# Linear attention and a gated MLP on one core: queries scaled at the cast, a new order of the first loads, filler matmuls, and no two-operand work on GpSimd

## The chip, the cores and the metric

The kernel runs on one core of a Trainium2 chip. The metric is the device time of one execution in microseconds. A core has five engines that run side by side: TensorE (PE in the profile; its weight loads are PEld), VectorE (DVE), ScalarE (ACT), GpSimd (POOL) and SyncE (SP). SP, ACT and POOL also issue DMA transfers, each into a queue of its own. Matmuls write to the eight banks of PSUM.

## The reference

Decayed linear attention in blocks of 64 rows, for 4 batches, 8 heads, 768 rows and a head size of 64, then an MLP over the 3072 rows of the result (512 to 2048 to 512, SiLU between).

```python
for b in range(nb):                                   # 12 blocks of 64 rows
    intra = (qb @ kb.T * Dmask) @ vb                  # lam**(i-j) for i >= j
    inter = (qb * lam_pow) @ kv_state                 # lam**(i+1)
    out[block] = intra + inter
    kv_state = lam**64 * kv_state + (kb * rev_pow).T @ vb
x = out.transpose(0, 2, 1, 3).reshape(B * S, H * D)   # 3072 x 512
h = x @ w_in                                          # 2048 wide
result = (h / (1 + exp(-h))) @ w_out
```

## The kernel before, in words

**Units and sets.** The rows of a batch are cut into six units of 128 rows, 24 in all. Two units are loaded as a set, three loads each (keys, queries, values, `raw`, 512 KB in float32). Sets 0 to 3 hold units 0 and 1 of one batch each and are "paired" (`prepare_2`, `first_2`, `second_2`); sets 4 to 11 hold one unit of two batches (`prepare`, `first_part`, `second_part`).

**Attention of one set.** Keys and queries are cast to bf16 (`kq`, on DVE or ACT, L313 and L315), values are scaled by powers of lambda (`vd`, L320, on DVE or POOL). TensorE turns `kq` into `kqT` (L442, through a PSUM bank `tr` and a copy) for sets 0 to 3; the rest are turned by a DMA transpose that SP issues (L622). TensorE then forms the states (`d_ps`, L463 and L647) and the scores (`st_ps`, L514 and L657). DVE masks the scores (`st`). The states run through a short chain on DVE (`y`, `xf`, `yf`), and the result is copied into block-diagonal tiles (`xe`, L313, L315, L317). TensorE adds scores times values ("outs", L538 and L679) and states times queries ("inter", L543 and L687) in `x_ps`. DVE takes that out of PSUM and multiplies it by `lam_xe`, the queries' power of lambda, into `xt`. In `first_2` the states stand ahead of the scores, and a chain (`after("b", ...)`) keeps that order on TensorE.

**MLP.** For each group of units, `product1` multiplies `xt` by w_in (L830, output `h_ps`) and ACT applies SiLU into `g` (L839). A group is one paired set (256 columns per matmul) or four units (512). For units 0 to 7, `product2_plain` multiplies `g` by w_out (L861, `o_ps`). For units 8 to 23, `product2` forms seven products in place of eight out of sums and differences of the blocks of `g` and of w_out (L1072). These sums (`s`, and `g` in place) are DVE's, except one of the four, which goes to POOL (`BY_POOL`). The last group's first product is formed the same way (`product1_spared`, L944).

**Weights.** w_in and w_out come in four quarters each, cast to bf16 on the way, issued by POOL (L364, L367). `SEQUENCE` sets the order of the first loads: "s0 i0 s1 i1 i2 s2 i3 o0 s3 o1 o2 o3 s4", where s is a set (issued by SP), i a quarter of w_in, o a quarter of w_out. The first quarter after a set is held by a gate: a small POOL copy (L331) that reads the set's first load, so POOL issues the quarter only once that load is there.

**Order.** Every piece of work is a task with a key (its priority), the engines that can do it and an assumed time on each, the tasks it depends on, and its buffers (`Buf`, from pools whose sizes stand in `POOLS`; "two", "one" and "att" are tickets that hold back how much is open at once). The `Planner` plays the tasks through with these times, a model of the load queues and the moment at which each engine begins, and writes down an order for each engine. The instructions are issued in that order; each engine works through its own list strictly in order.

Of the kernel before, what the change touches and what calls it, by code (L numbers as in the profile page):

```python
# [37 lines left out]
class Planner:  # L38

    LAT = {"PE": 0.23, "ACT": 0.06, "DVE": 0.06, "POOL": 0.08, "SP": 0.0}  # L40
    BEGIN = {"PE": 0.8, "ACT": 8.3, "DVE": 4.5, "POOL": 4.7, "SP": 0.8}
    FIRST, LAST, AHEAD = {"SP": 1.9, "ACT": 1.15, "POOL": 2.5}, 1.0, 0.75

    def __init__(self, pools):
        self.pools = {n: list(range(c)) for n, c in pools.items()}
        self.tasks = []

    def add(self, key, on, fn, deps=(), bufs=(), nbytes=0, kind=None, prior=(), late=0.0):
        key = key if isinstance(key, tuple) else (key,)
        t = Task(key, on, fn, deps, list(bufs) + [b.with_ for b in bufs if b.with_], nbytes, kind, prior, late)  # L50
        for b in t.bufs:
            b.left += 1
        self.tasks.append(t)
        return t

    def order(self):
# [14 lines left out]
        seq = 0  # L71
# [48 lines left out]
        while len(out) < len(self.tasks):  # L120
# [9 lines left out]
            for e in free:  # L130
# [8 lines left out]
                while ready[e]:  # L139
# [12 lines left out]
                    mine = now + t.on[e]  # L152
                    if any(max(free[o], now) + d < mine - 1e-9 for o, d in t.on.items() if o != e):
                        kept.append((key, i, t))
                        continue
# [4 lines left out]
                if took is None:  # L160
                    continue
# [5 lines left out]
                free[e] = now + t.on[e]  # L167
# [21 lines left out]
def kernel(  # L189
# [70 lines left out]
    row_i = const.tile([128, U], mybir.dt.int32, name="row_i")  # L260
    nc.gpsimd.iota(row_i, pattern=[[1, U]], base=-64, channel_multiplier=0)
# [20 lines left out]
    pose_2 = const.tile([128, 2], F32, name="pose_2")  # L282
    for a in range(2):
        nc.vector.tensor_scalar(pose_2[:, a:a + 1], iota_2, -1.0, 64.0 - a, op0=AL.mult, op1=AL.add)
    pose = const.tile([128, 1], F32, name="pose")
    nc.vector.tensor_scalar(pose, iota_p, -1.0, 64.0, op0=AL.mult, op1=AL.add)
    row = const.tile([128, U], F32, name="row")
    nc.vector.tensor_copy(row, row_i)
# [6 lines left out]
    lam_v = const.tile([128, H], F32, name="lam_v")  # L295
    lam_xe = const.tile([128, NP, U], F32, name="lam_xe")
    lam_be = const.tile([128, NP], F32, name="lam_be")
    lam_v2 = const.tile([128, H, 2], F32, name="lam_v2")
    for a in range(2):
        nc.scalar.activation(lam_v2[:, :, a], log_all, AF.Exp, scale=pose_2[:, a:a + 1])  # L300
    nc.scalar.activation(lam_v, log_all, AF.Exp, scale=pose[:, 0:1])
    for a in range(NP):
        nc.scalar.activation(lam_xe[:, a, :], row, AF.Exp, scale=log_lam[:, a:a + 1])
# [26 lines left out]
    def gated(key, load, i, tile):  # L330
        pool_task(add(key, {"POOL": 0.15}, lambda e: nc.gpsimd.tensor_copy(gate[:, i:i + 1], tile()), deps=load,  # L331
                      prior=pool_last[-1:]))
# [3 lines left out]
    raw = {}  # L336

    def load_set(key, si):
        n, b = sets[si][0]
        nb = 2  # L340
        rs = [Buf("ra" if si in (0, 3) else "rb") for _ in range(3)]
# [4 lines left out]
        def go(e, i):  # L346
            if n < PAIRED:
                tile_of(rs[i], [128, H, 2, 64], F32, "raw")
                nc.sync.dma_start(out=rs[i].tile.rearrange("p h e d -> p h (e d)"), in_=x[i])
            else:  # L350
                nc.sync.dma_start(out=tile_of(rs[i], [128, 2 * H, 64], F32, "raw"), in_=x[i])

        for i in range(3):
            ts.append([add((key, i), {"SP": 0.55}, lambda e, i=i: go(e, i), bufs=[rs[i]], nbytes=0.524,
                           kind=WIDE if n < PAIRED else SMALL, late=0.3 if si < FRESH else 3.0)])
        raw[si] = rs, ts
# [3 lines left out]
    def load_w(key, what, j):  # L360
        def go(e):
            if what == "i":
                cs = slice(512 * j, 512 * j + 512)
                nc.gpsimd.dma_start(out=w_in_bf[:, :, cs], in_=w_in_r[:, :, cs])  # L364
            else:
# [3 lines left out]
        wload[what, j] = pool_task(add((key, 0), {"POOL": 0.8}, go, [], [], 1.0486,  # L369
                                       LARGE, prior=pool_last[-1:], late=1.0))  # L370

    last, unit = None, None
    for m, x in enumerate(SEQUENCE.split() + [f"s{i}" for i in range(len(sets))]):
        j = int(x[1:])
        if x[0] == "s":
            if j not in raw:
                load_set(m - 100, j)
                unit = j
        else:
            if last != unit:  # L380
                rs, loads = raw[unit]
                gated((m - 100, -1), loads[0], unit, lambda b=rs[0]: b.tile[:, 0, 0, 0:1] if len(b.tile.shape) == 4 else b.tile[:, 0, 0:1])
                last = unit
            load_w(m - 100, x[0], j)
# [25 lines left out]
    def key_of(si):  # L410
        u = rank[sets[si][0]]
        return u - 4.0 if sets[si][0][0] == 0 else u - LEAD

    def prepare_2(o, rs, lk, lq, lv):
# [5 lines left out]
        def cast(e, i, a):  # L420
            copy(e, o.kq_of()[:, i, :, a], rs[i].tile[:, :, a, :].rearrange("p (m h) d -> p m h d", h=2))

        o.ck = [[add((s - 1.0, i), {"DVE": 0.43, "ACT": 0.63}, lambda e, i=i, a=a: cast(e, i, a), deps=(lk, lq)[i],
                     bufs=[rs[i], o.kq]) for a in range(2)] for i in range(2)]
# [7 lines left out]
        o.cv = [add((s - 0.8, 0), {"DVE": 0.7}, lambda e, a=a: scale_v(e, a), deps=lv, bufs=[rs[2], o.vd]) for a in range(2)]  # L432
# [19 lines left out]
    def first_2(o):  # L452
# [13 lines left out]
        td = add((s - 0.6, 0), {"PE": 0.45}, states, deps=o.cv + o.ck[0], bufs=d_ps + [o.kq, o.vd])  # L466
        after("b", td)
# [13 lines left out]
        def blocks(xe, i, src, t, buf):  # L481
            def go(e, r):
                if xe.tile is None:
# [6 lines left out]
        t0 = add((s - 0.9, 3), {"DVE": 0.42}, lambda e: tt(e, small(xf), d_ps[0].tile, rate, AL.mult), deps=[td], bufs=[d_ps[0], xf])  # L490
        o.xe_ready = blocks(o.xe_in, 0, lambda: xf.tile, t0, xf)
        t1 = add((s - 0.9, 4), {"DVE": 0.42}, lambda e: tt(e, small(y), d_ps[1].tile, xf.tile, AL.add), deps=[td, t0],
                 bufs=[d_ps[1], xf, y])
        t2 = add((s - 0.9, 5), {"DVE": 0.42, "POOL": 0.7}, lambda e: tt(e, xf_of(), y.tile, rate, AL.mult), deps=[t1], bufs=[y, xf_n])
        xf_t.append(t2)
        xe_t += blocks(xe_n, b0 % 2, xf_of, t2, xf_n)

# [6 lines left out]
        o.st_of = st_of  # L504
        deps = [t for t in o.turned]
        o.masked = []
        for g in range(2):
# [11 lines left out]
            for p in range(2):  # L519
# [5 lines left out]
                o.masked.append(add((s - 0.9, 0), {"DVE": 0.69}, mask, deps=[ts], bufs=[st_ps[g][p], o.st2[p]]))  # L525
        after("m", o.masked)

    def second_2(o):
# [21 lines left out]
        for c in range(2):  # L550
            def evac(e, c=c):
                tl = tile_of(xt[gi], [128, KI, 256], BF16, "xt")
                dst = tl[:, :, 128 * c:128 * c + 128].rearrange("p m (c e) -> p m e c", e=2)
                tt(e, dst, x_ps[c].tile, lam_xe.rearrange("p m (c e) -> p m e c", e=2), AL.mult)

            xt_done[gi].append(add((s - 0.9, 6), {"DVE": 0.7}, evac, deps=[(t0, t1)[c]], bufs=[x_ps[c], xt[gi]]))

    def prepare(si):
# [7 lines left out]
        o.kq, o.kqT, o.vd, o.st = Buf("kq"), Buf("kqT"), Buf("vd"), Buf("st")  # L566
# [6 lines left out]
        def kq_of():  # L573
            return tile_of(o.kq, [128, nb, 2, NP, 2, 64], BF16, "kq")

        def kqT_of():
            return tile_of(o.kqT, [128, nb, 2, NP, U], BF16, "kqT")
# [9 lines left out]
        def cast(e, j, i):  # L587
            src = rs[i].tile[:, j * H:j * H + H, :].rearrange("p (m h) d -> p m h d", h=2)
            dst = kq_of()[:, j, i]
            copy(e, dst, src)  # L590

        ck = [[add((s - 1.0, i), {"DVE": 0.43, "ACT": 0.63}, lambda e, j=j, i=i: cast(e, j, i), deps=(lk, lq)[i],
                   bufs=[rs[i], o.kq]) for i in range(2)] for j in range(nb)]
        after("k", [t for ts in ck for t in ts])
# [4 lines left out]
        cv = [add((s - 0.8, 0), {"DVE": 0.7} if si < FRESH else {"POOL": 1.25, "DVE": 0.7}, lambda e, j=j: scale_v(e, j),  # L599
# [5 lines left out]
        if si < TURNED:  # L605
            for j in range(nb):
                bank = Bank(fills=False)

                def turn(e, j=j, bank=bank):
                    t = tile_of(bank, [128, 2, NP, U], BF16, "tr")  # L610
                    for i in range(2):
                        for m in range(NP):
                            nc.tensor.transpose(t[:, i, m, :], kq_of()[:, j, i, m], ident)

                tr = add((s - 0.7, j), {"PE": 0.46}, turn, deps=ck[j], bufs=[bank, o.kq])
                for i in range(2):
                    o.turned.append(add((s - 1.0, 2), {"DVE": 0.43, "ACT": 0.6},
                                        lambda e, j=j, i=i, bank=bank: copy(e, kqT_of()[:, j, i], bank.tile[:, i]),
                                        deps=[tr], bufs=[bank, o.kqT]))
        else:  # L620
            def dma_turn(e):
                nc.sync.dma_start_transpose(kqT_of().rearrange("p b i m s -> p (b i m) s"),  # L622
                                            kq_of().rearrange("p b i m h d -> p (b i m h d)"))
# [4 lines left out]
    def first_part(o):  # L628
# [12 lines left out]
        def states(e):  # L641
            for j in range(nb):
                for m in range(NP):
                    for c in halves_of_d:
                        r = halves[c]
                        for p, rp in enumerate(halves):
                            nc.tensor.matmul(d_of(c)[rp, j, m, :], lhsT=o.kq_of()[r, j, 0, m, p, :],  # L647
# [3 lines left out]
        def scores(e):  # L651
            for j in range(nb):
                for m in range(NP):
                    for p, rp in enumerate(halves):
                        t = tile_of(st_ps[p], [128, nb, NP, 64], F32, "st_ps")
                        for c, r in enumerate(halves):
                            nc.tensor.matmul(t[r, j, m, :], lhsT=o.kqT_of()[rp, j, 0, m, r], rhs=o.kqT_of()[rp, j, 1, m, r],  # L657
# [6 lines left out]
    def second_part(o):  # L664
# [18 lines left out]
        def inter(e):  # L683
            for c in range(2):
                for j in range(nb):
                    for m in range(NP):
                        nc.tensor.matmul(x_of(c)[:, j, m, :], lhsT=o.xe[c].tile[:, (bs[0] + j) % 2, m, :],  # L687
                                         rhs=o.kqT_of()[:, j, 1, m, halves[c]],
# [484 lines left out]
```

## Time and profile before

| what | us |
|---|---|
| time, median of 3 runs (lowest, highest) | 207.66 (207.39, 208.27) |
| profiled execution | 207.82 |
| its span, first to last instruction | 206.1 |
| PE busy | 187.0 (91%) |
| DVE busy | 134.8 (65%) |
| ACT busy | 107.4 (52%) |
| POOL busy | 52.4 (25%) |
| mean granted clock of TensorE | 0.989 |

The page cuts the span into 40 slices of 5.15 us and gives the busy share of each engine in each slice as one digit, in tenths. PEclk is the granted TensorE clock in tenths of full speed. A chain row gives the start, the length and the work that the end of the program hung on. In the timeline a bracket gives the idle time ahead of an instruction and what ended it. Matmuls overlap, so the mean duration of one is longer than the time that it takes from its neighbours. The queue q0 carries what POOL issues, q1 what SP issues, q10 what ACT issues; q0's bytes are counted after the cast to bf16.

### The profile page before, as it was taken

The numbers are of one execution on the slowest core, as the hardware profiler recorded it, in microseconds if no ns is written. First come the engines' busy times: TensorE is split into PE (matmuls) and PEld (weight loads), VectorE is DVE, ScalarE is ACT, GpSimd is POOL, SyncE is SP. The second block draws the span as 40 slices with busy tenths as digits, with TensorE's granted clock in tenths as the row PEclk, the third lists the DMA queues.
The fourth block names the chain that finished last, engine by engine and source line by source line (L and its number), as shares of the span: only waits on it lengthen the run. The fifth ranks groups of instructions, "written<-read, shape, count | busy, mean of one in ns | idle before, by whom it ended". The sixth has DMA issues, their size and how long they took to land.

```text
span 206.1 us, 5719 instructions
## 1 busy us (share of the span) xinstructions
PE 187.0 (91%) x2445; PEld 132.9 (64%) x2464; DVE 134.8 (65%) x249; ACT 107.4 (52%) x195; POOL 52.4 (25%) x76
## 2 busy tenths in 40 slices
PE   0459399999999999999999999998999999999993
PEld 0347288786667565544578648474675778888882
DVE  6488632767950467716989953999758995665411
ACT  3637267874336453375734492745615453766420
POOL 7231400401130111222565013346003221222200
PEclk9999889999999999999999999999999999999999
DMA  3999999999999999999999999905101110102213
GB/s 99 292 253 260 228 222 265 235 199 214 228 238 249 156 216 231 238 219 195 263 213 234 203 213 240 244 7 117 39 3 54 51 54 0 54 0 102 88 52 118
DMA packets 88617, 33.92 MB, mean 165 GB/s; under 512 B 67088, under 2 KB 87568, under 8 KB 88592
## 3 DMA queue, kind: packets, MB, share of 16 engines
q1 hardware_dynamic: 79232, 23.60, 57.3%
q0 software_dynamic: 4224, 4.19, 12.2%
q10 hardware_dynamic: 5136, 5.77, 8.7%
q8 instruction: 19, 0.31, 0.7%
q14 instruction: 6, 0.05, 0.1%
HBM read 27.27 MB, written 6.29 MB: 163 GB/s over the span
## 4 chain that ended last, share of the span: by engine, by line
PE 82%; DMA 8%; DVE 7%; issue 1%; ACT 0%; POOL 0%; POOLq 0%; DVEq 0%
PE h_ps L830 31%; PE o_ps L1072 22%; PE o_ps L861 13%; PE h_ps L944 6%; DMA w_in_bf<-in_moe_w_in_dram 5%; DMA raw<-in_k_dram 3%; PE x_ps L687 2%; DVE s L320 2%; PE tr L442 2%; DVE g L320 1%; PE d_ps L647 1%; PE x_ps L679 1%; PE st_ps L657 1%; PE x_ps L538 1%; DVE kq L315 1%
## 5 line engine op out<-in xcount | busy, mean ns | idle before, releaser
L830 PE MATMUL h_ps<-xt,w_in_bf 128*128 128x256 bf16 (+1 forms) x439 | 75.7, 322 | 4.7 <-DMA w_in_bf<-in_moe_w_in_dram 3.3
L839 ACT ACTIVATE g<-h_ps 128x512 bf16<-128x512 f32 x80 | 47.1, 594 | 45.7 <-PE h_ps L830 45.0
L830 PEld LDWEIGHTS <-w_in_bf 128*128 128x128 bf16 x448 | 43.7, 99 | 30.1 <-DMA w_in_bf<-in_moe_w_in_dram 3.5
L861 PE MATMUL o_ps<-w_out_bf,g 128*128 128x512 bf16 x118 | 29.7, 379 | 0.6 <-issue 0.2
L320 POOL TENSOR_TENSOR s<-g,s 128x512 bf16<-128x512 bf16 x16 | 19.0, 1188 | 43.1 <-DVE s L320 26.8
L320 DVE TENSOR_TENSOR st<-st_ps,tri 128x512 bf16<-128x512 f32 x32 | 20.5, 681 | 11.2 <-PE st_ps L657 11.2
L1072 PEld LDWEIGHTS <-g 128*128 128x128 bf16 x256 | 24.9, 98 | 4.4 <-ACT g L839 0.3
L320 DVE TENSOR_TENSOR xt<-x_ps,lam_xe 128x512 bf16<-128x512 f32 x24 | 15.9, 699 | 15.2 <-PE x_ps L687 9.5
L1072 PEld LDWEIGHTS <-s 128*128 128x128 bf16 x192 | 18.7, 98 | 2.6
L861 PEld LDWEIGHTS <-g 128*128 128x128 bf16 x128 | 12.1, 98 | 12.0
L320 POOL TENSOR_TENSOR vd<-raw,lam_v 128x512 bf16<-128x512 f32 x10 | 13.3, 1334 | 25.1 <-DMA raw<-in_v_dram 19.7
L313 ACT ACTIVATE kq<-raw 128x512 bf16<-128x512 f32 x27 | 16.2, 621 | 2.1 <-DMA raw<-in_q_dram 1.6
L320 DVE TENSOR_TENSOR osb<-o_ps,m 128x512 f32<-128x512 f32 (+1 forms) x15 | 8.7, 583 | 10.9 <-ACT m L313 6.8
L1072 PE MATMUL o_ps<-wsum,g 128*128 128x256 bf16 x128 | 15.3, 272 | 0.0
L1072 PE MATMUL o_ps<-w_out_bf,s 128*128 128x256 bf16 x128 | 15.3, 273 | 0.0
L442 PE MATMUL tr<-ident,kq 128*128 128x128 bf16 x64 | 7.0, 260 | 8.8 <-POOL gate L331 6.9
L1072 PE MATMUL o_ps<-w_out_bf,g 128*128 128x256 bf16 x128 | 15.0, 273 | 0.0
L320 DVE TENSOR_TENSOR s<-g 128x512 bf16<-128x512 bf16 x16 | 8.2, 510 | 10.4 <-ACT g L839 6.6
L313 ACT ACTIVATE m<-o_ps 128x512 f32<-128x512 f32 (+1 forms) x14 | 7.0, 503 | 11.4 <-PE o_ps L1072 11.4
L320 DVE TENSOR_TENSOR vd<-raw,lam_v 128x512 bf16<-128x512 f32 x14 | 9.2, 681 | 5.0 <-DMA raw<-in_v_dram 5.0
L313 ACT ACTIVATE osb<-o_ps 128x512 f32<-128x512 f32 (+1 forms) x12 | 6.7, 562 | 10.4 <-PE o_ps L861 6.5
L315 DVE CAST kq<-raw 128x512 bf16<-128x512 f32 x21 | 9.1, 451 | 3.8 <-DMA raw<-in_k_dram 2.0
(88 smaller groups left out, 215.1 us busy)
## 6 DMA issues: line engine op xcount, KB each, us to landing
raw<-in_k_dram SPq DMA_DIRECT2D x12, 512.0 KB, 8.2
raw<-in_q_dram SPq DMA_DIRECT2D x12, 512.0 KB, 8.5
raw<-in_v_dram SPq DMA_DIRECT2D x12, 512.0 KB, 8.0
out_dram<-osb ACTq DMA_DIRECT2D x20, 256.0 KB, 3.6
w_in_bf<-in_moe_w_in_dram POOLq DMA_DIRECT2D x4, 512.0 KB, 10.0
w_out_bf<-in_moe_w_out_dram POOLq DMA_DIRECT2D x4, 512.0 KB, 11.7
out_dram<-osb ACTq DMA_DIRECT2D x4, 128.0 KB, 1.7
out_dram<-osb SPq DMA_DIRECT2D x4, 128.0 KB, 1.7
```

The source lines that it names most:

```text
L313: nc.scalar.activation(o, i, AF.Copy)
L315: nc.vector.tensor_copy(o, i)
L320: (nc.vector if e == "DVE" else nc.gpsimd).tensor_tensor(o, a, b, op=op)
L442: nc.tensor.transpose(t[:, m, a], o.kq_of()[:, i, m, a], ident)
L538: nc.tensor.matmul(t[rh, m], lhsT=o.vd_of()[r, 2 * m + h, a, :], rhs=o.st_of(h)[r, m, a], start=m == 0 and a == 0, stop=True, skip_group_c ...
L647: nc.tensor.matmul(d_of(c)[rp, j, m, :], lhsT=o.kq_of()[r, j, 0, m, p, :], rhs=o.vd_of()[r, j, 2 * m + p, :], start=j == 0 and m == 0, sto ...
L687: nc.tensor.matmul(x_of(c)[:, j, m, :], lhsT=o.xe[c].tile[:, (bs[0] + j) % 2, m, :], rhs=o.kqT_of()[:, j, 1, m, halves[c]], start=False, s ...
L830: nc.tensor.matmul(t[:, j, :], lhsT=w_in_bf[:, ko, 128 * (m1 + j):128 * (m1 + j) + 128], rhs=xt[gi].tile[:, ko, :], start=(ko == 0), stop= ...
L839: nc.scalar.activation(t[:, half * per:half * per + per], bank.tile, AF.Silu)
L861: nc.tensor.matmul(t, lhsT=g.tile[:, j, 128 * gp:128 * gp + 128], rhs=w_out_bf[:, ko, :], start=(ko == 0), stop=(ko == KO - 1))
L944: nc.tensor.matmul(t[:, j, :], lhsT=W[w]()[:, k2, f:f + 128], rhs=X(r)[:, k2, :], start=first and j == 0 and k2 == 0, stop=True, skip_grou ...
L1072: nc.tensor.matmul(t[:, i_, :], lhsT=src(j)[:, k2, 128 * r:128 * r + 128], rhs=W[w]()[:, 2 * j + k2, :], start=first and i_ == 0 and j == ...
```

## The change

- *Queries first, scaled at the cast.* In sets 0 to 3 the queries are loaded ahead of the keys. In all sets the queries are multiplied by their power of lambda while they are cast (a DVE instruction with two operands, where DVE or ACT made a plain cast). `lam_xe` goes; `x_ps` is taken out by a plain copy, on ACT or DVE. The powers are arranged so that scores with scaled queries and scaled values need no other mask.
- *Scores ahead of states* in sets 0 and 1.
- *First loads.* The new sequence is "s0 i0@0.2 s1 i1a@0.2 i1b i2 i3 o0 o1 s2@1.2 o2 o3 s3 s4". "@0.2" holds a load until set 0's third load, the values, is there. Quarter 1 comes in two halves. Set 2 is held on SP by a tiny DMA that waits for set 1's values; every later load of SP is kept in order behind it.
- *Fillers.* Where the plan leaves TensorE idle from 9.6 to 24 us, it puts in four 128-column matmuls on the identity (without a gap until 17 us, then one per 0.3 us), into a PSUM bank that is held for it until 24 us. Their results aren't read.
- *GpSimd.* It no longer scales values, makes no sum of `s` and no product for `xf`; DVE does these. It keeps the `xe` copies, the gates and the weight loads.
- *Set 4* is turned by TensorE (`TURNED` 4 to 5).
- *Last group's first product.* One of the seven products accumulates onto a copy in PSUM of another, in place of a sum on DVE; SiLU is taken from PSUM; the sums of w_in are due sooner.
- *Planner.* New assumed times, a bias against DVE, slower TensorE before 15.5 us; `two` tickets doubled from 4 to 8, so that the first four units can have their second products open at once.

The core of the diff:

```diff
-    LAT = {"PE": 0.23, "ACT": 0.06, "DVE": 0.06, "POOL": 0.08, "SP": 0.0}
-    BEGIN = {"PE": 0.8, "ACT": 8.3, "DVE": 4.5, "POOL": 4.7, "SP": 0.8}
+    LAT = {"PE": 0.23, "ACT": 0.16, "DVE": 0.15, "POOL": 0.08, "SP": 0.0}
+    OVERLAP = {"ACT": 0.1, "DVE": 0.09}
+    BEGIN = {"PE": 0.8, "ACT": 7.7, "DVE": 4.5, "POOL": 4.7, "SP": 0.8}
+    BIAS = {"DVE": 0.2}
+    SLOW, SLOWER = 15.5, 1.8
+    DENSE, THIN, REST = (9.6, 17.0), 24.0, 0.3
...
                 if took is None:
+                    if e == "PE" and self.filler and self.DENSE[0] <= now < self.THIN:
+                        if fill is None:
+                            fill = Buf("bank")
...
+                        if now >= self.DENSE[1] and now < rested + self.REST - 1e-9:
+                            heapq.heappush(events, rested + self.REST)
+                            continue
+                        if waiting[e] and waiting[e][0][0] < now + 0.1:
+                            continue
+                        free[e] = rested = now + 0.22 * (2 if now < self.SLOW else 1)
...
-    FRESH, TURNED, ALONE, LEAD = 4, 4, 6, 6.5
-    SEQUENCE = "s0 i0 s1 i1 i2 s2 i3 o0 s3 o1 o2 o3 s4"
+    FRESH, TURNED, ALONE, LEAD = 4, 5, 6, 6.5
+    SEQUENCE = "s0 i0@0.2 s1 i1a@0.2 i1b i2 i3 o0 o1 s2@1.2 o2 o3 s3 s4"
...
-                 xt2=2, xt4=2, g=18, s=12, m=3, osb=3, one=3, two=4, att=6)
-    BY_POOL, IN_BY_POOL, PLAIN, SPARED = (4,), (), 8, 1
+                 xt2=2, xt4=2, g=18, s=12, m=3, osb=3, one=3, two=8, att=6, sp=2)
+    BY_POOL, IN_BY_POOL, PLAIN, SPARED = (), (), 8, 1
+    CASTING, SUMS_AFTER, HURRY, SUMS_ON, HOLD, ONTO = 12, 16, 0.0, 9.0, 1, 24
+    OPEN, FILLED, SCALED = 4, True, ()
+    QUERIES = (0, 1, 2, 3)
+    SCORED, SOON, VD_ON, HALVED = (0, 1), 3, {"DVE": 0.7}, 0
...
-    for a in range(NP):
-        nc.scalar.activation(lam_xe[:, a, :], row, AF.Exp, scale=log_lam[:, a:a + 1])
+    for i, t in ((1, lam_q2), (0, lam_v2)):
+        for a in range(2):
+            nc.scalar.activation(t[:, :, a], log_all, AF.Exp, scale=pose_2[:, i, a:a + 1])
...
         def cast(e, j, i):
-            copy(e, dst, src)
+            if i:
+                tt(e, dst, src, lam_q[:, :, None].to_broadcast([128, H, 64]), AL.mult)
+            else:
+                copy(e, dst, src)
...
-        cv = [add((s - 0.8, 0), {"DVE": 0.7} if si < FRESH else {"POOL": 1.25, "DVE": 0.7}, lambda e, j=j: scale_v(e, j),
+        cv = [add((s - 0.8, 0), VD_ON, lambda e, j=j: scale_v(e, j),
...
-        td = add((s - 0.6, 0), {"PE": 0.45}, states, deps=o.cv + o.ck[0], bufs=d_ps + [o.kq, o.vd])
-        after("b", td)
...
+        if o.si not in SCORED:
+            rest()
...
+        if o.si in SCORED:
+            rest()
         after("m", o.masked)
...
-                tt(e, dst, x_ps[c].tile, lam_xe.rearrange("p m (c e) -> p m e c", e=2), AL.mult)
-            xt_done[gi].append(add((s - 0.9, 6), {"DVE": 0.7}, evac, ...
+                copy(e, dst, x_ps[c].tile)
+            xt_done[gi].append(add((s - 0.9, 6), {"ACT": 0.75, "DVE": 0.75}, evac, ...
...
-        tf = add((s - 0.9, 4), {"DVE": dcost, "POOL": 0.25 + w / 560}, ...
+        tf = add((s - 0.9, 4), {"DVE": dcost}, ...
...
+            if x[0] == "s":
+                held = [add((m - 100, -1), {"SP": 0.15}, lambda e, g=gates, tile=tile: nc.sync.dma_start(
+                    out=gate[0:1, g:g + 1], in_=tile()[0:1]), deps=loads[i], bufs=[rs[i]], prior=sp_last[-1:])]
+            else:
+                gated((m - 100, -1), loads[i], gates, tile, rs[i])
...
-        bank, two, two2, osb = Buf("bank"), Buf("two"), Buf("two"), Buf("osb")
+        twos = [Buf("two") for _ in range(2 if u < OPEN else POOLS["two"] // 2)]
...
-            b1, c1 = keep("kqT", [m1])
-            m2 = product(1, R, "A12", "B21", True, [])
-            e11 = total_of(lambda w=wide_of: w()[:, :, lo], wide, b1, [m2, c1])
+            c1 = add((u0 - eager, 5), {"ACT": 0.6, "DVE": 0.69}, lambda e, P=P, R=R, f=bank_of: copy(e, f(R), f(P)), ...
+            m2 = product(1, R, "A12", "B21", False, [c1])
+            s11 = silu((low, lo), lambda R=R, f=bank_of: f(R), [m2], [R])
...
+    def filler(b):
+        def go(e):
+            t = tile_of(b, [128, 4, 128], F32, "ones")
+            for i in range(4):
+                nc.tensor.matmul(t[:, i, :], lhsT=ident, rhs=ident, start=i == 0, stop=True, skip_group_check=True)
```

More of the change, by code (lines that the diff above doesn't have):

```diff
@@ L119, in order @@
                 arm(t)
[L120 removed]
+        fillers, fill, rested = 0, None, 0.0
+        while len(out) < len(self.tasks) + fillers:
             if not events:
@@ L340, in load_set @@
         nb = 2
-        rs = [Buf("ra" if si in (0, 3) else "rb") for _ in range(3)]
+        rs = [Buf("rb") if si >= CASTING and i == 0 else None if si >= CASTING and i == 1 else Buf("ra" if si in (0, 3) else "rb")
+              for i in range(3)]
         ts = []
@@ L367, in go @@
                 nc.gpsimd.dma_start(out=w_out_bf[:, ks, :], in_=w_out_r[:, ks, :])
-        wload[what, j] = pool_task(add((key, 0), {"POOL": 0.8}, go, [], [], 1.0486,
-                                       LARGE, prior=pool_last[-1:], late=1.0))
+        t = pool_task(add((key, 0), {"POOL": 0.8}, go, [], [], 0.5243 if part else 1.0486,
+                          HALF if part else LARGE, prior=pool_last[-1:], late=1.0))
+        wload.setdefault((what, j), []).append(t)
+        for h in ("a", "b") if not part else part:
+            wload[what, j, h] = t
@@ L375 @@
         if x[0] == "s":
-            if j not in raw:
-                load_set(m - 100, j)
-                unit = j
-        else:
[L380 to L384, printed above, removed]
+            load_set(m - 100, j)
+            if behind:
+                raw[j][1][QUERIES.count(j)][0].prior += held
@@ L1051, in product2, with products_of @@
         for part in ((0,), (1,)) if last else ((0, 1),):
-            products_of(units, s, A, part, last, eager)
-    def products_of(units, s, A, part, last, eager):
+            products_of(units, s, A, part, last, eager, u0)
+    def products_of(units, s, A, part, last, eager, u0):
         np_ = len(part)
         P, R = Buf("bank"), Buf("bank")
-        held = [P, R] + [Buf("two") for _ in range(2 * np_)]
+        held = [P, R] + [Buf("two") for _ in range((POOLS["two"] // 4) * (1 if u0 == PLAIN and HOLD else np_) * 2)]
         late = part[0] * 2 / 7 if last else 0.0
@@ L1125 @@
         product1(gi)
+    for t in waits:
+        t.deps += gs[0, 0][2]
+        t.bufs.append(gs[0, 0][0])
+        gs[0, 0][0].left += 1
     if SPARED:
```

263 lines of the change are left out of this document (160 added, 103 removed).

## The prediction

> **What bounds the kernel now.** I read the page's 40 slices first, then busy time by stretch, then the chain that ended last, then the timeline and the DMA queues of the first 40 us.
>
> ```profile
> ## 2 busy tenths in 40 slices
> PE   0459399999999999999999999998999999999993
> PEclk9999889999999999999999999999999999999999
> DMA  3999999999999999999999999905101110102213
> ```
>
> TensorE (PE) is full from the sixth slice to the last but one; only the first five slices have room. The busy time by stretch puts numbers to it (start:end, length, PE busy, clock, DMA share, GB/s):
>
> ```profile
> 5.00:24.00 19.00, 10.32 (x213) 1.00 1.18 260
> 24.00:202.60 178.60, 176.68 (x2233) 0.99 0.77 158
> ```
>
> From 24.0 us on PE idles 1.92 us in 178.6. So the end is the moment from which PE is dense, plus the work left then, plus a tail of 3.6 us (206.1 - 202.5) that the change leaves alone. Time is to be won by doing PE work before 24 us, by running it at the full clock, or by having less of it. The chain (start, us, what) shows what holds PE until 24:
>
> ```profile
> 13.71 10.23 DMA w_in_bf<-in_moe_w_in_dram
> 23.94 0.05 issue
> 23.99 3.41 PE h_ps L830 x16
> 27.40 0.70 PE x_ps L538 x21
> 28.09 0.33 PE x_ps L543 x4
> 28.42 0.45 PE tr L442 x8
> 28.87 1.75 PE h_ps L830 x16
> ```
>
> The second quarter of w_in is issued at 13.71 and lands at 23.9. Until then PE has done set 0's attention, 16 matmuls on the first quarter (17.92 to 19.7), and set 1's transposes, states and scores (until 20.65); then it stands for 3.3 us. It goes on at half speed: the same 16 matmuls take 3.41 us at 23.99 and 1.75 at 28.87, and the granted clock of 24 to 28 us is 0.57. The loads behind it, as the two load queues moved them from 21 to 24 us (packets, MB, share):
>
> ```profile
> q0 software_dynamic: 432, 0.43, 83.7%
> q1 hardware_dynamic: 431, 0.22, 35.5%
> ```
>
> q0 (weights, issued by POOL) moves 0.143 MB/us, so a quarter of 0.524 MB needs 3.65 us, while q1 (queries, keys, values, issued by SP) falls to 0.073 MB/us; from 7 to 9 us, alone, q1 moved 0.56 MB, 0.28 per us.
>
> **The start after the change.** The first quarter's gate (POOL) now waits for set 0's values, not its first load. q1 has moved set 0's 1.57 MB by 8.85 us; the first load was moved by 5.2 and its reader started at 6.44, so I add 1.2: values at 10.1, weights issued at 10.4 instead of 7.12. The first quarter's data began 2.6 us after its issue: 13.0 plus 3.65 is 16.7, visible at 17.4 with half a us for landing (the row of its whole way, 7.8 us, gives 18.2; the second quarter's, 10.2, gives 20.6). I take 17.4, since q1 has less left to compete with. Quarter 1, now in halves, and all that POOL issues behind it without a gate follow at q0's rate: 19.2 and 21.0, quarter 2 at 24.7, quarter 3 at 28.3, the first two quarters of w_out at 32 and 35.6. Seven issues of 0.75 to 0.96 us keep POOL until 16.4; the block copies that it shared with ACT go to ACT then (0.42 each).
>
> Is set 0 ready at 17.4? Queries come first and are cast and scaled on DVE: two instructions of 0.68 (row vd<-raw,lam_v, same shapes), 6.46 to 7.8. The keys land where the queries did, by 8.6; casts 0.6, transposes 0.94, copies 0.60, scores 1.08 lead to 12.0. Before, the scores waited behind states that waited for vd until 11.98, and the masks began at 12.99; now they begin at 11.5, so the 2.48 us of masks end at 14.0. Outs 1.07, inter 0.61, and the evacuation as a plain copy on both engines (0.7, was 1.35 on DVE) end at 16.4, against 17.87 before. The weights are then the later of the two, by 1 us.
>
> From 17.4 PE has set 0 on quarters 0 and 1 (3.5 us). Set 1's queries and keys are moved by 13 us, and its transposes and scores fit ahead; of its values 0.33 MB is left at 13, which takes 5 us at 0.07: landed at 19.3, vd 20.6, states 21.0, xe 21.9, inter 22.3, evacuated 23.1, and 0.8 us of its matmuls fit before 24.
>
> **The sum**, against the profiled execution (206.1 us span, 1.72 outside it, 207.82; the median of the runs shown is 207.66, so the two are one).
> - Cold clock at 24 gone, 3.41 - 1.75: -1.66 (bounds 0 and -1.66). Fillers, four matmuls on the identity each, keep PE busy. The trace has none; eight 128-column matmuls take 0.45 warm and seven 0.94 cold, so one costs 0.22 to 0.54. It costs nothing where PE would stand; where a real burst is ready early, it waits for one: a dozen bursts, at most 2.6 us warm.
> - Set 0 on quarter 1 done before 24: -1.75 (0 to -1.75).
> - Set 1's outs and inter before 24: -1.03; 0.8 of its matmuls: -0.80 (together 0 to -1.83).
> - Set 4 turned on PE: 16 transposes at 0.45 for 8, +0.90 (0.88 to 1.2). Its four copies (0.42 on DVE, 0.60 on ACT) lie beside dense PE. One of eight DMA transposes goes (6.8 us from issue to landing), near 57 us, where PE doesn't wait.
> - The one later stall of size, 0.69 at 139.9: -0.4 (next paragraph).
> - Bursts put out of place by a filler or by the new order: +0.4, a choice between 0 and 2.6.
>
> 207.82 - 1.66 - 1.75 - 1.83 + 0.90 - 0.4 + 0.4 = 203.5.
>
> On the transposes the row and a rule differ: the group row says 260 ns each, the chain 0.45 us for eight, because neighbours overlap. The Trainium skill (TensorE: Matmul & The Clock Gate, Part 4) puts a transpose at about 275 ns in a kernel and says that the full clock doesn't engage for it; by that the 16 would cost an estimated 4.4 us. The chain's eight in 0.45 inside dense PE don't bear it out.
>
> **GpSimd without two-operand work.**
>
> ```profile
> 105.82 0.68 DVE L320 TENSOR_TENSOR w_out_bf<-w_out_bf 128x1024 bf16<-128x1024 bf16 x1
> 106.98 1.20 POOL L320 TENSOR_TENSOR s<-g,s 128x512 bf16<-128x512 bf16 x1 [1.96 <-DVE s L320]
> 107.09 1.64 DVE L320 TENSOR_TENSOR w_out_bf<-w_out_bf 128x1024 bf16<-128x1024 bf16 x1
> ```
>
> The same DVE instruction takes 0.68 alone and 1.64 beside POOL's: DVE stands until POOL is done. So of POOL's 16 s sums (19.0 us) and 10 vd (13.3), DVE has long paid a part. To DVE go 16 x 0.42, 10 x 0.68 and one xf of 0.68: +14.2; queries always on DVE, 24 x 0.68, less its half of them now (about 11 x 0.45): +11.4. From it go the waits for POOL: g 16 x 0.19, s 16 x 0.09, xf 5 x 0.22, 3 more of w_out, xsum and xe: -8.6; half of 24 evacuations to ACT, -8.4; in the last group's first product four sums of 0.69, which become accumulation onto a copied bank, -2.8. DVE goes from 134.8 to about 141 of 203 us and ACT stays near 107, by the same rows. Neither bounds the whole; the chains through DVE lose POOL's 1.19 for 0.42. Whether 100 to 140 us stands it is a rival. The new wait, one accumulating product behind that copy (0.6), has other products queued beside it; PE sees it only when those run out.
>
> No cost: the kq layout, dropped row and lam_xe (ACT 1.3 us in the prologue, replaced by three Exp of 0.29), w_in's sums sooner, larger pools, and options set so that they touch nothing (CASTING 12, ONTO 24, HALVED 0). The new planner costs only reorder; a bad order shows as the stalls of the rivals.
>
> **Rivals.**
> - *The fillers don't do what they say.* PE takes them in order, not at planned times: a clump runs off early, PE then stands and goes cold as at 23.99. Against it: 0.3 us spacing after 17. The -1.66 fails and displaced bursts cost about 0.6 more: 205.8.
> - *DVE becomes the bound.* From 100 to 140 us DVE is busy 33.0 of 40. Moved there: 8 s and 5 vd, 6.8; queries 3.7; off it, waits 4 and evacuations 2.6: 36.9 of 40. The stall at 139.9 comes at the end of such a chain (DVE busy 9.73 of 10). If each of four groups adds 0.9, PE loses 3.5: 207.0.
> - *Slower: set 2 is held and PE runs dry at 34 to 40 us.* SP's queue waits for set 1's values, and sets 2, 3 and every later load stand behind. Set 2 starts at 21, gets 0.07 MB/us until w_out's second quarter is through at 35.6, is complete near 38 and evacuated at 42; before, this was at 43.1. PE, being ahead, finishes the first two sets' w_in matmuls at 33.7. It then lives on w_out: 6.9 us with two quarters, and 2.4 of set 2's attention, until 43. That needs four output units open at once (the tickets are doubled for it). If banks or g tiles forbid it, or w_out lands late, PE stands from 35.7 to 42: +6.3, 209.8. It decides as soon as more than 4.3 us of that work is missing.
> - *Transposes at their recorded length*, 16 x 0.26: 206.8.
>
> **Chances.** Forecast (201.8 to 204.9) 0.50; better than that, if set 1 comes sooner, 0.06; fillers 0.18; DVE 0.12; dry PE 0.12; transposes 0.02. The 80% range leaves out the dry case and a little at the bottom: 201.0 to 207.4. A measurement here can tell about 0.5%, 1.0 us. Faster by more: 0.50 + 0.06 + 0.18 + a third of DVE = 0.78; within: 0.08; slower: 0.14.
>
> **What would show it.** Right: first h_ps near 17.4 at 109 ns each, weights as releaser; no 3 us gap before 24 and a clock near 1.0 from 24 to 28; the 128 first matmuls of sets 0 and 1 done by 34 (now 120 of them by 40.7); no DVE sum at 1.6. Wrong: first h_ps after 19, a clock of 0.5 anywhere after 17, PE waiting for set 2 near 40, or stalls behind DVE after 100.

## The result and the profile after

| | before | after |
|---|---|---|
| median of 6 runs (lowest, highest), us | 207.64 (206.48, 208.75) | 204.45 (204.29, 204.71) |
| ratio, 95% interval | | 0.9846 (0.9815 to 0.9877) |
| profiled execution, us | 207.82 | 204.46 |
| its span, us | 206.1 | 202.4 |
| end of the last matmul, us | 202.52 | 198.66 |
| DVE, ACT, POOL busy, us | 134.8, 107.4, 52.4 | 135.5, 114.2, 21.8 |

The changed kernel is 3.2 us faster, clear of the half per cent that can be told here; forecast were 4.3 us less, 203.5. Below, every experiment is given with its ratio to the kernel before on the same chip; a second measurement of the changed kernel gave 0.9857 (0.9801 to 0.9914), 204.52 us. What an experiment lost, in us, is its median less that of the changed kernel; worked out from the ratios, which allow for the chip, most losses come out up to 0.7 us higher or lower. Of the four runs of experiment 2 (213.22, 213.32, 212.92 and 209.81 us) its ratio leaves out the two longest.

The page of the changed kernel, the same rows as before:

```profile
## 2 busy tenths in 40 slices
PE   0588999999999999999999999999999999999992
PEclk9999999999999999999999999999999999999998
DMA  3999999999999989999999999948001111003313
```

PE is now full from the fifth slice, the two slices of low clock (8) near 24 us are gone, and a slice is 5.06 us where it was 5.15. The busy time by stretch (start:end, length, PE busy, clock, DMA share, GB/s):

```profile
5.00:24.00 19.00, 14.93 (x296) 1.00 1.24 251
24.00:198.70 174.70, 173.13 (x2199) 1.00 0.77 160
```

After 24 us PE idles 1.57 us, 1.92 before. Not all of the 14.93 us ahead of 24 is useful work: about 3.1 are fillers, 32 matmuls from 9.67 to 17.3 us, which is eight bursts where the prediction allowed for a dozen. The timeline of PE around 20 us (start, us, engine, line, operation, count, idle before and its releaser):

```profile
18.72 1.05 PE L905 MATMUL h_ps<-xt,w_in_bf 128*128 128x256 bf16 x8
19.70 0.44 PE L534 MATMUL d_ps<-vd,kq 64*64 64x64 bf16 x32
20.18 1.91 PE L905 MATMUL h_ps<-xt,w_in_bf 128*128 128x256 bf16 x16
22.01 0.64 PE L614 MATMUL x_ps<-st,vd 64*64 64x128 bf16 x32
...
23.07 1.04 PE L905 MATMUL h_ps<-xt,w_in_bf 128*128 128x256 bf16 x8
24.36 0.82 PE L905 MATMUL h_ps<-xt,w_in_bf 128*128 128x256 bf16 x6 [0.26 <-ACT xt L342]
```

All 32 matmuls of set 0 on quarters 0 and 1 are done by 24 us, at full clock (1.91 for 16, where the 16 at 23.99 took 3.41), with set 1's attention between them. There is no gap, though the first h_ps starts later than before (18.72 against 17.92). From 24.36 on nothing of size stands still. What set 24.36 is the chain of the changed kernel:

```profile
17.26 0.64 DVE xt L344
17.89 0.42 DVE kqT L344
18.32 1.20 DVE vd L349 x2
19.52 2.40 DVE st L349 x4
...
23.68 0.64 ACT xt L342
24.32 0.04 issue
24.36 6.28 PE h_ps L905 x56
```

It is DVE's list, not a load: set 0's second half is taken out at 17.26 to 17.89, then come set 1's values and its four masks. The loads were there: set 1's values at 15.05, the first quarter of w_in at 18.4, the two halves of quarter 1 at 19.6 and 21.5.

**Where the 3.86 us at the last matmul come from** (202.52 - 198.66): cold clock -1.66, set 0 on quarter 1 -1.75, set 1's outs and inter -1.03, 16 transposes more +0.90, a start 0.37 later (24.36 against 23.99), idle time after that -0.61 (1.92 to 1.31). The sum is -3.78; the other 0.08 isn't accounted for. The tail after the last matmul is 0.16 longer and the time outside the span 0.34, which leaves 3.36 in the profiled executions.

### The profile page after: what moved, and what is told of

Same layout as the page of the kernel before. It is cut to its first block, busy times and chain, and to the rows that moved or that the text cites. A ratio compares the mean times of both kernels' runs of the same rounds, so it can differ in the third digit from the quotient of the medians.

```text
span 202.4 us, 5779 instructions
## 1 busy us (share of the span) xinstructions
PE 188.1 (93%) x2494; PEld 135.0 (67%) x2512; DVE 135.5 (67%) x269; ACT 114.2 (56%) x207; POOL 21.8 (11%) x48
## 4 chain that ended last, share of the span: by engine, by line
PE 84%; DVE 6%; DMA 4%; ACT 3%; issue 1%; DVEq 0%; SPq 0%
PE h_ps L905 33%; PE o_ps L1153 22%; PE o_ps L940 14%; PE h_ps L1023 6%; DMA raw<-in_k_dram 3%; DVE st L349 2%; PE x_ps L767 2%; PE d_ps L727 1%; PE tr L513 1%; PE x_ps L759 1%; DVE vd L349 1%; PE st_ps L737 1%; DMA out_dram<-osb 1%; ACT xt L342 1%; DVE kqT L344 1%
## 5 line engine op out<-in xcount | busy, mean ns | idle before, releaser
L905 PE MATMUL h_ps<-xt,w_in_bf 128*128 128x256 bf16 (+1 forms) x440 | 73.7, 317 | 0.7 <-ACT xt L342 0.3
L940 PE MATMUL o_ps<-w_out_bf,g 128*128 128x512 bf16 x118 | 28.6, 379 | 0.8 <-issue 0.5
L349 DVE TENSOR_TENSOR kq<-raw,lam_q 128x512 bf16<-128x512 f32 x24 | 16.3, 698 | 6.2 <-DMA raw<-in_q_dram 4.5
L342 ACT ACTIVATE xt<-x_ps 128x512 bf16<-128x512 f32 x16 | 9.7, 631 | 12.3 <-PE x_ps L767 9.2
L349 DVE TENSOR_TENSOR vd<-raw,lam_v 128x512 bf16<-128x512 f32 x24 | 15.7, 682 | 0.7 <-DMA raw<-in_v_dram 0.7
L1153 PE MATMUL o_ps<-wsum,g 128*128 128x256 bf16 x128 | 15.1, 273 | 0.0
L349 DVE TENSOR_TENSOR s<-g 128x512 bf16<-128x512 bf16 x16 | 7.2, 447 | 10.8 <-ACT g L917 8.1
L513 PE MATMUL tr<-ident,kq 128*128 128x128 bf16 x64 | 6.1, 241 | 7.7 <-DVE kq L349 7.5
L342 ACT ACTIVATE kq<-raw 128x512 bf16<-128x512 f32 x14 | 8.4, 624 | 4.5 <-DMA raw<-in_k_dram 4.0
L346 POOL CAST xe<-xf 64x256 bf16<-64x256 f32 (+1 forms) x8 | 5.1, 640 | 49.4 <-DVE xf L349 39.3
L513 PEld LDWEIGHTS <-kq 128*128 128x128 bf16 x64 | 4.6, 107 | 8.4 <-DVE kq L349 7.9
```

The costliest lines, as they stand in the source:

```text
L342: nc.scalar.activation(o, i, AF.Copy)
L346: nc.gpsimd.tensor_copy(o, i)
L349: (nc.vector if e == "DVE" else nc.gpsimd).tensor_tensor(o, a, b, op=op)
L513: nc.tensor.transpose(t[:, m, a], o.kq_of()[:, i, m, a], ident)
L905: nc.tensor.matmul(t[:, j, :], lhsT=w_in_bf[:, ko, 128 * (m1 + j):128 * (m1 + j) + 128], rhs=xt[gi].tile[:, ko, :], start=(ko == 0), stop= ...
L940: nc.tensor.matmul(t, lhsT=g.tile[:, j, 128 * gp:128 * gp + 128], rhs=w_out_bf[:, ko, :], start=(ko == 0), stop=(ko == KO - 1))
```

## The experiments

**1. No fillers.** All engines' lists but PE's stay word for word.

```diff
-    OPEN, FILLED, SCALED = 4, True, ()
+    OPEN, FILLED, SCALED = 4, False, ()
```

> The changed kernel without fillers; every other instruction and order stays. Theory as predicted (the fillers keep the clock up): a stretch of granted clock near 0.5 and 16 or so matmuls at twice their time come back, +1.7 us, 206.1. Rival (the fillers are not needed, because the new order leaves no gap of 3 us and PE's own work keeps the clock): clock stays near 1.0 from 18 us on, 204.3 to 204.6.

Measured: 205.61 us, ratio 0.9903 (0.9865 to 0.9941): 1.1 to 1.2 us lost (1.0 to 1.2 by the ratios; the intervals just touch). Its chain:

```profile
18.19 1.10 PE st_ps L588 x30
19.29 1.82 PE h_ps L905 x8
21.11 0.57 PE d_ps L534 x17
21.68 2.37 PE h_ps L905 x16
```

The first 8 matmuls take 1.82 us, not 0.87, and the first five of the next 16 are as slow: single matmuls start 213 ns apart until 22.65 us and 109 ns apart from 22.79 on. From there the clock stays up. So the fillers are not superfluous, but it isn't they that save the cold stretch (matmuls at half speed) at 24: without them PE's own work brings the clock up at 22.7 us, and with no gap of 3 us left it stays up. What the fillers win is the time before 22.7. The measured time lies between the two that were expected. The busy times by stretch give a clock of 1.00 throughout, because the trace holds no record of the clock before 22.70 us (before 13.29 in the changed kernel); the spacing of the matmuls shows it.

**2. GpSimd's two-operand work given back**, the order of PE's work unchanged.

```diff
-    BY_POOL, IN_BY_POOL, PLAIN, SPARED = (), (), 8, 1
+    BY_POOL, IN_BY_POOL, PLAIN, SPARED = (4,), (), 8, 1
...
-        cv = [add((s - 0.8, 0), VD_ON, ...
+        cv = [add((s - 0.8, 0), {"POOL": 1.25, "DVE": 0.7}, ...
...
-        tf = add((s - 0.9, 4), {"DVE": dcost}, ...
+        tf = add((s - 0.9, 4), {"DVE": dcost, "POOL": 0.25 + w / 560}, ...
```

> The changed kernel with GpSimd's two-operand work given back (values of sets 4 to 11, one of four sums of s, xf); TensorE's order is the same. Start theory (the gain is made before 24 us): +0.4 to +0.7 us, one stall of PE behind DVE after 100 us returns, DVE sums of 1 us and more beside GpSimd's. Relief theory (the gain is made by freeing the chains through DVE): +2 us or more.

Measured: 209.81 us in the fastest of four runs, ratio 1.018 (1.0068 to 1.0293): 5.3 us lost there and over 8 in the other three, far over the 0.4 to 0.7. The profiled execution took 213.22 us, and 1.4 us of that is a late start: its first loads landed 1.5 us later, so set 1's matmuls begin at 25.74, not 24.36. Its rows show how time is lost after that, not how much in the fastest run. PE's waits in it (us in total, times, longest):

```profile
PE h_ps L905 <- DVE st L349: 2.3, 1, 2.3
PE o_ps L1153 <- DVE osb L349: 2.3, 1, 2.3
```

DVE and POOL ahead of the first of these waits:

```profile
138.51 5.58 POOL L349 TENSOR_TENSOR s<-g,s 128x512 bf16<-128x512 bf16 x2 [1.70 <-DVE s L349]
142.04 2.60 DVE L349 TENSOR_TENSOR wsum<-w_in_bf 128x1024 bf16<-128x1024 bf16 x2
144.05 2.94 POOL L349 TENSOR_TENSOR vd<-raw,lam_v 128x512 bf16<-128x512 f32 x2
144.56 2.97 DVE L349 TENSOR_TENSOR wsum<-wsum,w_in_bf 128x1024 bf16<-128x1024 bf16 x2
```

The same instructions in the changed kernel:

```profile
137.84 1.88 DVE L349 TENSOR_TENSOR wsum<-w_in_bf 128x1024 bf16<-128x1024 bf16 x3
139.64 1.28 DVE L349 TENSOR_TENSOR wsum<-wsum,w_in_bf 128x1024 bf16<-128x1024 bf16 x2
```

Two DVE sums take 2.97 us beside POOL and 1.28 alone, and two of POOL's take 5.58 where one that starts just ahead of DVE's next instruction (at 135.63) takes 1.18: each holds up the other. The masks behind these sums on DVE come late, and PE stands for them; after the first of the two waits the granted clock falls, to 0.94 from 140 to 170 us. The Trainium skill (SBUF — State Buffer, Who interferes with whom) says that a DVE instruction with two inputs in SBUF contends with a GpSimd instruction that reads SBUF, over ports that one of them holds alone; the rows agree.

**3. The old order of the first loads**, with fillers and all else of the change.

```diff
-    SEQUENCE = "s0 i0@0.2 s1 i1a@0.2 i1b i2 i3 o0 o1 s2@1.2 o2 o3 s3 s4"
+    SEQUENCE = "s0 i0@0.1 s1 i1@1.1 i2 s2 i3@2.1 o0 s3 o1@3.1 o2 o3 s4"
```

> The changed kernel with the old order and gates of the first loads (first quarter behind the set's first load, no hold of set 2), fillers and all else kept. Start theory: the second quarter lands at 23 or later again, set 0's 16 matmuls on it fall back behind 24 us and part of set 1's too: +1.8 to +2.8 us, 206.2 to 207.2; with fillers the clock stays up. Relief theory: within 0.7 us.

Measured: 208.48 us, ratio 1.0028 (0.9985 to 1.007): the whole gain gone. The chain:

```profile
9.78 15.61 DMA raw<-in_q_dram
25.39 0.02 issue
25.41 0.69 DVE kq L349
26.11 0.34 DVE xf L349
...
27.34 0.75 ACT xt L342
28.09 0.04 issue
28.13 2.78 PE h_ps L905 x24
```

The loss, 3.6 to 4.0 us, is larger than expected, and comes by another way than the late quarter. That quarter landed at 21.7; set 0's 16 matmuls on it ran at 24.62 and 25.72 all the same, because PE's list has set 1's work ahead of them. Nor did the fillers keep the clock up throughout (0.93 over the first 24 us). Set 2's queries, not held, share the queues with the weights and land at 25.4; their cast stands in DVE's list ahead of set 1's xf, so set 1 is evacuated at 28.1. A load that comes later than the plan thinks blocks an engine that has other work.

**4. Four tickets for open output units instead of eight.**

```diff
-    ... one=3, two=8, att=6, sp=2)
+    ... one=3, two=4, att=6, sp=2)
```

> The changed kernel with the tickets for open output units back at 4, so that only two of the first four units can be open on TensorE at once. Dry-PE rival (PE, ahead of set 2, lives on w_out's first quarters): PE stands between 34 and 42 us, +2 to +6 us. If other work fills that stretch: less than 0.5 us.

Measured: 207.53 us, ratio 0.9985 (0.9955 to 1.0015): 2.7 to 3.1 us lost. The longest of PE's waits, and the chain, at the place that the prediction named:

```profile
41.15 0.21 PE L614 MATMUL x_ps<-st,vd 64*64 64x128 bf16 x1 [0.77 <-DVE st L349]
...
36.61 8.22 DMA w_out_bf<-in_moe_w_out_dram
44.83 0.04 issue
44.87 0.59 PE o_ps L940
```

With two units open PE has used up what the first two quarters of w_out allow by 39.5 us. Then it has only set 2's attention, stands four times between its masks (1.7 us together, 40 to 43), and goes on with w_out when the third quarter lands at 44.83. The changed kernel has products with w_out to put between the masks. From 28 to 60 us PE idles 2.4 of 32, where the changed kernel idles 0.5, and its clock is 0.95, where it was 1.00. So the rival of the dry PE was real, and the doubled tickets are what keeps it away.

**5 to 7. The hold, set 4, set 5.** One constant each:

```diff
-    ... s2@1.2 o2 o3 s3 s4"          # 5: no hold
+    ... s2 o2 o3 s3 s4"
-    FRESH, TURNED, ALONE, LEAD = 4, 5, 6, 6.5
+    FRESH, TURNED, ALONE, LEAD = 4, 4, 6, 6.5   # 6: set 4 by DMA
+    FRESH, TURNED, ALONE, LEAD = 4, 6, 6, 6.5   # 7: set 5 by TensorE too
```

> The changed kernel without the hold of set 2 (its loads follow set 1's in SP's queue at once). Set 2's loads then share the queues with the w_in quarters from 14 us on. Start theory: quarters 1 to 3 land 1 to 2 us later but set 2 comes sooner; +0 to +1 us. Rival (the hold was what brought quarter 1 in before 24 us): +1.7 us or more.

Measured: 205.51 us, ratio 0.9925 (0.9889 to 0.9961), +1.0 us on the same chip as the second measurement of the changed kernel. PE waits 0.85 us for a w_in load at 24.87. The hold is worth 1 us by the medians, the upper end of the first expectation, and 1.4 by the ratios.

> The changed kernel with set 4 turned by a DMA transpose again. By the chain's rows (8 transposes in 0.45 us): 0.9 us less work on TensorE, -0.9 us, unless set 4 then comes late and PE stands near 60 to 75 us. By the group row's 260 ns each: -4 us. Rival (the transpose occupied the load queue where the data were needed): +0.5 us or more.

Measured: 206.59 us, ratio 0.9964 (0.9932 to 0.9996): 2.1 us lost, not 0.9 won. Yet TensorE's price is what the rows said; this is the changed kernel's chain, set 4's transposes:

```profile
59.33 0.45 PE tr L693 x8
...
60.65 0.45 PE tr L693 x8
```

Without them PE has no wait over 0.3 us between 40 and 90 us, so set 4 is not late either. The loss lies elsewhere: the plan comes out otherwise from there on, and in the profiled execution PE idles 2.26 us from 100 to 140, where the changed kernel idles 0.21, behind DVE's and ACT's copies. (That execution took 208.17 us, the longest of ten, and begins 1.5 us late besides: set 1's matmuls start at 25.90.) So the loss seems to be the price of a new plan, and not of the transpose; no run separates the two.

> The changed kernel with set 5 turned by TensorE as well. By the two chain rows of set 4 (0.45 us for 8 transposes): +0.9 us. Queue theory (a DMA transpose between loads delays the sets behind it, which is why undoing set 4's cost 2 us): within 0.3 us or faster. If the new plan alone decides: anything, with stalls of PE behind DVE after 100 us.

Measured: 206.07 us, ratio 0.9947 (0.9908 to 0.9985), +1.6 us. In its profile the last matmul ends 0.74 us later than in the changed kernel, near the 0.9 of the rows, and the tail after it is 1.2 us longer. Queue theory falls: one DMA transpose less again didn't help.

**8. The kernel before with GpSimd's two-operand work on DVE.**

```diff
-    BY_POOL, IN_BY_POOL, PLAIN, SPARED = (4,), (), 8, 1
+    BY_POOL, IN_BY_POOL, PLAIN, SPARED = (), (), 8, 1
...
-        cv = [add((s - 0.8, 0), {"DVE": 0.7} if si < FRESH else {"POOL": 1.25, "DVE": 0.7}, ...
+        cv = [add((s - 0.8, 0), {"DVE": 0.7}, ...
...
-        tf = add((s - 0.9, 4), {"DVE": dcost, "POOL": 0.25 + w / 560}, ...
+        tf = add((s - 0.9, 4), {"DVE": dcost}, ...
```

> The kernel before with only GpSimd's two-operand work moved to DVE. If that work was already costly there: -2 us or more. As the prediction priced it (one stall of 0.69 us at 139.9): -0.3 to -0.7 us. Since GpSimd's work given back to the changed kernel cost 5 us or more, the theory now is that it hurts only where DVE also scales the queries: here within 0.7 us of the kernel before.

Measured: 208.76 us, ratio 1.0041 (1.0006 to 1.0077): slightly slower, barely clear of the noise. The sums are fast now (no two-operand DVE instruction over 1.10 us, where the longest was 1.95), but PE waits behind DVE as before, at another instruction near 139 us:

```profile
PE o_ps L1072 <- DVE osb L320: 0.9, 1, 0.9
```

So this part alone gains nothing. Experiment 2 says that the rest of the change needs it.

**9. The kernel before with quarter 1 sooner.**

```diff
-    SEQUENCE = "s0 i0 s1 i1 i2 s2 i3 o0 s3 o1 o2 o3 s4"
+    SEQUENCE = "s0 i0 i1 s1 i2 i3 o0 o1 s2 o2 o3 s3 s4"
```

> The kernel before with only its sequence of first loads changed to 's0 i0 i1 s1 i2 i3 o0 o1 s2 o2 o3 s3 s4' (quarter 1 issued with quarter 0; no hold, no fillers, nothing else). Start theory: quarter 1 is there before 20 us, PE has work before 24 and does not stand 3.3 us, so the cold clock of 24 to 28 goes too: -1.7 to -3.4 us. Rival (set 1 comes later instead, and the new order pays only together with the hold, the fillers and the earlier scores): within 1 us of the kernel before.

Measured: 209.28 us, ratio 1.0145 (1.0078 to 1.0212): slower. PE's timeline:

```profile
18.00 3.57 PE L830 MATMUL h_ps<-xt,w_in_bf 128*128 128x256 bf16 x16 [0.90 <-DVE xt L320]
...
27.20 1.92 PE L830 MATMUL h_ps<-xt,w_in_bf 128*128 128x256 bf16 x16 [0.94 <-DMA w_in_bf<-in_moe_w_in_dram]
...
30.93 1.90 PE L861 MATMUL o_ps<-w_out_bf,g 128*128 128x512 bf16 x7 [0.99 <-DMA w_out_bf<-in_moe_w_out_dram]
```

The gap of 3.3 us is gone, and still nothing is won: the first 16 matmuls run cold (3.57), set 1 comes later (its states at 29.05, before at 19.76), and PE then stands for quarters of w_in and w_out, with two units open. The rival that the order pays only together with the rest holds for this order; it is near to the new one, but has neither its gate on set 0's values nor its halved quarter.

**10. States first again in sets 0 and 1.**

```diff
-    SCORED, SOON, VD_ON, HALVED = (0, 1), 3, {"DVE": 0.7}, 0
+    SCORED, SOON, VD_ON, HALVED = (), 3, {"DVE": 0.7}, 0
```

> The changed kernel with states ahead of scores again in sets 0 and 1. If the first quarter of w_in (landed at 18.0) binds the first matmul: within 0.5 us of the changed kernel. If the chain through DVE binds (masks of set 0 and 1 later by the 1.2 us that vd takes): +1 to +1.5 us.

Measured: 205.82 us, ratio 0.9942 (0.9912 to 0.9971): 1.3 us lost (1.8 to 2.0 by the ratios). PE's timeline:

```profile
18.86 0.32 PE L534 MATMUL d_ps<-vd,kq 64*64 64x64 bf16 x16 [0.28 <-DVE vd L349]
18.99 0.64 PE L588 MATMUL st_ps<-kqT 64*64 64x128 bf16 x32
19.56 2.79 PE L905 MATMUL h_ps<-xt,w_in_bf 128*128 128x256 bf16 x24
```

The first h_ps starts at 19.56, not 18.72; the weights have been there since 18.4 (not 18.0, as the expectation has it). Ahead of it on PE stand set 1's states, which wait for `vd` in DVE's list: DVE's chain binds. The profiled execution is the shortest of eight (204.85), and its last matmul ends only 0.4 us later than in the changed kernel; where the longer ones lose the rest isn't shown.

**11. Queries not scaled at the cast**: plain casts, `lam_xe` back, `x_ps` multiplied by it on DVE.

```diff
-                tt(e, dst, src, lam_q[:, :, None].to_broadcast([128, H, 64]), AL.mult)
+            copy(e, dst, src)
...
-                copy(e, dst, x_ps[c].tile)
+                tt(e, dst, x_ps[c].tile, lam_xe.rearrange("p m (c e) -> p m e c", e=2), AL.mult)
```

> The changed kernel with the queries cast plainly (DVE or ACT) and the power of lambda multiplied on DVE when x_ps is taken out, as before. DVE's load is the same to 1 us either way (24 x 0.68 moved). As priced: set 0 and set 1 are evacuated 0.6 us later, +0.3 to +0.8 us. Rival (the DVE chains after 100 us bind): +1.5 us or more. Other rival (no effect): within 0.3.

Measured: 206.25 us, ratio 0.9958 (0.9942 to 0.9974): 1.75 us lost, more than priced, and not after 100 us (PE idles 0.11 of 40 there). It is at the start:

```profile
22.25 0.42 PE L617 MATMUL x_ps<-st,vd 64*64 64x128 bf16 x16 [0.52 <-DVE vd L356]
...
23.58 0.45 PE L537 MATMUL d_ps<-vd,kq 64*64 64x64 bf16 x32
...
26.38 2.78 PE L909 MATMUL h_ps<-xt,w_in_bf 128*128 128x256 bf16 x24 [0.82 <-DVE xt L356]
```

Set 1's first matmul starts 2.0 us later than at 24.36. In DVE's list the second half of set 1's values now stands behind its four masks (19.21 to 21.60), and the states (23.58), the short chain and the second half of the evacuation (25.60 to 26.34, on DVE alone) follow from that.

No version here beats the changed kernel. Three parts of the change were not taken out singly: the queries' place ahead of the keys, the last group's first product and the planner's new times.

**The second measurement of the changed kernel.**

> The changed kernel once more, as the yardstick of this chip: 0.9846 of the kernel before, as found first; every theory expects the same.

Measured: 0.9857, as said above.

## Why the prediction was right, and where its size was off

- *What bounds the kernel, and where the time is to be won*: right. The gain is made before 24 us, as the sum above shows and as experiment 3 does: with the old order of the loads nothing of it is left. Of the signs named ahead, the gap and the low clock after 24 us are gone, no two-operand DVE instruction takes over 1.09 us, and 120 of the first 128 matmuls of sets 0 and 1 are done by 34.6 us, where it was 40.7; the last eight, behind products with w_out, follow only at 37.2.
- *Cold clock, -1.66*: right as a size, wrong in its reason. The prediction gave it to the fillers; experiment 1 has no cold stretch at 24 us without them either, because the new order leaves no gap there. The fillers are worth 1.1 to 1.2 us by another way: without them the clock comes up at 22.7 us, and the first 13 matmuls with w_in run at half speed, which the prediction didn't see. So the term came out right partly by luck. The rival of the useless fillers falls.
- *Set 0 on quarter 1, -1.75*, and *set 1's outs and inter, -1.03*: right.
- *0.8 of set 1's matmuls before 24*: this step failed. It became a start 0.37 later, 1.2 us in all. The prediction had set 1's values land at 19.3; they were there by 15.1, when SP's hold passed (from 13 to 14 us q1 still moved 0.25 MB, and q0 0.03). But it let vd, states and the evacuation follow as if DVE were free, and left out of set 1's line the 2.4 us of masks that stand behind vd in DVE's list. For the same reason set 0 was ready at 17.9, not 16.4: set 1's queries, `xf` and a copy of set 1's `kqT` stood in DVE's list ahead of its second half. The first quarter of w_in, forecast for 17.4, landed at 18.4. The first matmul began at 18.72, when set 1's scores, ahead of it in PE's list, were through, and not on the weights' arrival. The prediction's order of events (weights last) held, by 0.5 us and not by 1.
- *Set 4 on PE, +0.90*: right to the row, two times 0.45 us. The longer price, by the group row, falls. That undoing it cost 2 us seems a matter of the plan; experiment 6 leaves open which of its stalls are due to DVE's order alone.
- *The later stall, -0.4, and bursts out of place, +0.4*: together -0.61. But the reason was half wrong: GpSimd's work moved by itself gained nothing (experiment 8). In the changed kernel, where DVE also scales the queries, giving it back costs 5 us or more (experiment 2). The prediction priced the relief against the kernel before and not against the kernel that it ends up in.
- *DVE as the bound*: it didn't come. From 100 to 140 us DVE is busy 33.9 of 40, not 36.9, and over the whole 135.5 us, not about 141; ACT has 114.2, not 107, as it took 16 of the 24 evacuations and not half. With POOL's work back (experiment 2) PE does wait behind DVE.
- *PE running dry near 40 us*: it didn't come, because four units can be open at once; with two it came, at 40 to 45 us, and cost 3 us, not 6.3.
- *Tail and time outside the span*, taken as unchanged: +0.5 together. This and the failed step (1.2), less the 0.6 that later idle time shrank by, make up the distance from 4.3 to 3.36, but for 0.1.

## What to carry to other kernels

Where one engine is full to the end, look for the moment at which it becomes full, and follow each set up to that moment through the list of every engine that it passes, DVE's above all: an instruction queued there for the next set counts like a wait. A bundle of edits is not the sum of its parts: a load order near to the new one, alone, lost 1.5%, and GpSimd's relief alone 0.4%; taken out of the whole, the new order costs 1.8% and the relief about 3%. Give back work to a second engine only after looking at which rows become longer beside it.

## What the runs showed of the hardware

The two load queues can take turns by packets, not by bytes. From 21 to 24 us of the changed kernel (packets, MB, share):

```profile
q0 software_dynamic: 424, 0.42, 81.8%
q1 hardware_dynamic: 423, 0.22, 34.9%
```

It was 432 to 431 in the kernel before and is 577 to 577 from 24 to 28 us here. Since q0's packets carry 1 KB after the cast and q1's 512 B, q1 gets a third of the bytes written in these stretches. It isn't so always: from 24 to 28 us of the kernel before the counts are 483 and 950, and no run here shows why. The Trainium skill (DMA: Bandwidth & Descriptors, Queues, rings and completion order) has the engines take turns between queues by packet, and its packet can hold several descriptors; the equal counts agree if that packet is the one that the profile counts, which no run here shows. The prediction only took over the rates and had not seen where they come from.
